# Token stage of a memory-attention gradient: products over two segments at once, with spread weights

## The chip, the cores and the metric

The kernel runs on one core of one Trainium2 chip. The core has five engines that work from queues of their own: TensorE (PE; its weight loads are listed as PEld), VectorE (DVE), ScalarE (ACT), GpSimd (POOL) and SyncE (SP, which here only issues DMAs). The metric is the device time of one execution in microseconds (us), less being better. The kernel before took 5357.48, 5364.2 and 5371.53 us in three runs; the median is 5364.2.

## The reference, cut to what matters

A gated mix of two attentions over 2048 tokens of width 576 is computed, and all its gradients. Attention A has 32 heads of 18 columns with one shared key and value. Attention B works in 64 segments of 32 tokens; each segment sees 8 memory rows ahead of its own tokens, and its output at the memory rows is the memory of the next segment. The change touches B, and in B only the tokens (not the memory rows, which are done in a serial chain elsewhere):

```
for s in range(n_seg):                               # 64 segments of 32 tokens
    xs = x[:, s * seg_len:(s + 1) * seg_len, :]
    h = concatenate([mem, xs], axis=1)               # 8 memory rows + 32 tokens
    q, k, v = einsum('btd,dhe->bhte', h, Wq), ...    # 32 heads of 128
    scores = where(mask, einsum('bhqe,bhke->bhqk', q, k) * scale, -1e9)
    p = softmax(scores)
    o = einsum('bhqe,...', p, v)                     # 'bhqk,bhke->bhqe'
    o = einsum('bhte,hed->btd', o, Wo)
    mem = o[:, :M, :]; outs.append(o[:, M:, :])
...
out = g * a + (1 - g) * b                            # g = sigmoid(x . gate_w)
grads = vjp(grad_out)                                # of x, all weights, mem0, gate_w
```

For the token queries the stage in question computes, head by head, the probabilities P, the output o = P v, and in the gradient dS (the gradient of the scores) and dq = dS k, with the memory rows' share added.

## The kernel before

The program runs in stages that follow each other: preparation; projections of the tokens; the forward chain of memory rows, woven with a pass of attention A; the token stage (`b_bulk`); the backward chain of memory rows, woven with A's second pass; the remaining gradients of B; the weight gradients; the end of A. Only the token stage is touched.

**Its steps.** A step t is four heads of one tile of 128 tokens, that is of four segments; 16 tiles by 8 groups of heads make 128 steps. A step's work is cut into 23 small stages (`st_QT`, `st_S`, `st_R` and so on), which are run as a software pipeline: the list `order` near line 913 holds pairs (n, stage), and turn t of the loop runs each stage in the order of the list for step t - n. There is no scheduler behind it: each engine's queue holds its instructions in exactly the order in which the list calls them. So a stage's place in the list sets its place in each queue that it uses.

**The stages that matter here**, with the engine that does them (the number is that of the list):

- `st_M` (2): DVE clears masked entries of the exponentials x_E.
- `st_QT`, `st_KT` (0), `st_OT` (4), `st_GT` (2), `st_VT` (2): PE transposes four 128x128 blocks of q, k, o, dO, v into a PSUM tile x_tr, of which there are two buffers, used in turn; then DVE (q, k, o) or ACT (dO, v) copies it out as x_qT, x_kT, x_oT, x_dOT, x_vT. PE can begin a transpose once the copy before last has let its buffer go.
- `mem_T`: PE transposes the memory columns of P and dS, DVE copies them out (x_mT).
- `st_B0`, `st_B1` (5): PE multiplies o by the output weights, into x_b.
- `st_R` (2): DVE sums x_E to x_l and inverts to x_r, POOL multiplies x_E by x_r to x_P.
- `st_D` (3): PE forms dO v transposed into x_D; DVE makes x_X (P times it) and its sums x_dl.
- `st_Y` (4): POOL makes x_Y (P times x_dl) and x_dS = x_X - x_Y.
- `st_T` (3) and `st_DT` (5): `transp`, line 741, has DVE transpose the 32x32 blocks of the token part of P and dS to x_PT and x_DT.
- `st_Om`, `st_Qm`: PE multiplies the memory part, one 128x512 product each, into the PSUM tile x_po.
- `st_O` (3) and `st_Q` (5): `attend`, line 764, adds the token part: for each of four heads and each of four segments a product of the segment's 32x32 block by its 32x128 values (v or k), and ACT copies x_po out to x_o or x_dq.

The products of `attend` lie on the diagonal of the PE array: `diag_mm` (line 269) puts segment r in rows and columns 32r to 32r + 32. The blocks of one head stand under each other in x_PT, [128 partitions, 32 columns], so each product takes 32 partitions of it as its weights.

DMAs: SP loads q, k, v, dO every four turns and stores P, dS, o, dq; the stores are collected in a list and issued at the end of the next turn. `self.tmask` (line 173) is a constant of [128, 2, 32] that holds 1 where the segment's number, modulo 2, is the middle index.

Of the kernel before, what the change touches and what calls it, by code (L numbers as in the profile page):

```python
# [10 lines left out]
ALU = mybir.AluOpType  # L11
AX = mybir.AxisListType
BF16 = mybir.dt.bfloat16
# [3 lines left out]
P = 128  # L17
# [29 lines left out]
class Kern:  # L47
# [221 lines left out]
    def diag_mm(self, out, i, lhsT, rhs, start, stop):  # L269
        for r in range(4):  # L270
            b = slice(32 * r, 32 * r + 32)
            self.mm(out[b, i, :], lhsT=lhsT[b], rhs=rhs[b], start=start, stop=stop, tp=(32 * r, 32 * r))

    def m_rows(self, t, c):
        return t[32 * c:32 * c + 8].rearrange("p u e -> p (u e)")
# [388 lines left out]
    def b_bulk(self, wp, vp, kp, sp, psum):  # L664
        nc = self.nc
# [75 lines left out]
        def transp(x, nm):  # L741
            o = sp.tile([P, 4, 32], BF16, name=nm, bufs=2)
            nc.vector.transpose(o[:].rearrange("p i k -> p (i k)"), x.rearrange("p i k -> p (i k)"))
            return o

        def mem_T(t):
            u = [(0, t - 3, "P"), (1, t - 5, "dS")]
# [11 lines left out]
        def attend_m(t, w, m):  # L759
            po = sc["po" + w, t] = psum.tile([P, 4, P], F32, name="x_po", bufs=2)  # L760
            self.mm(po[:].rearrange("p i e -> p (i e)"), lhsT=sc.pop((w + "mT", t)), rhs=m.rearrange("p i e -> p (i e)"),
                    start=True, stop=False)

        def attend(o, t, w, PT, v):
            po = sc.pop(("po" + w, t))
            for i in range(4):
                self.diag_mm(po, i, PT[:, i, :], v[:, i, :], False, True)
            nc.scalar.copy(o, po[:])

        def trans(t, w, nb):  # L770
            tt, g, r, d = view(t)
            pt = psum.tile([P, 4, P], BF16, name="x_tr", bufs=2)
            for i in range(4):
                self.tr(pt[:, i, :], d[w][:, 4 * (g % 4) + i, :], P)
            o = sp.tile([P, 4, P], BF16, name=f"x_{w}T", bufs=nb)
            self.evac(o[:], pt[:], use="s" if w in ("dO", "v") else "v")
            sc[w + "T", t] = o

        st_QT = lambda t: trans(t, "q", 2)
        st_KT = lambda t: trans(t, "k", 2)  # L780
        st_GT = lambda t: trans(t, "dO", 3)
        st_VT = lambda t: trans(t, "v", 3)
# [37 lines left out]
        def st_T(t):  # L820
            sc["PT", t] = transp(view(t)[3]["P"][:, t % 4, 0], "x_PT")

        st_Om = lambda t: attend_m(t, "P", mB["v"][t // 4 % 2][:, t % 4])
        st_Qm = lambda t: attend_m(t, "dS", mB["k"][t // 4 % 2][:, t % 4])

        def st_O(t):
            tt, g, r, d = view(t)
            o = chunk(t, "o", [P, 16, P], 2)
            attend(o[:, r, :], t, "P", sc.pop(("PT", t)), d["v"][:, r, :])
            store(t, self.xtok["o"], o)  # L830
# [11 lines left out]
        def st_B(t, a):  # L842
            tt, g, r, d = view(t)
            oT = sc["oT", t]
            if g == 0 and a == 0:
                pb[tt] = psum.tile([P, 2, 512], F32, name="x_b", bufs=1)
            for i in (2 * a, 2 * a + 1):
                for hf in range(2):
                    self.mm(pb[tt][:, hf, 0:288], lhsT=oT[:, i, :], rhs=self.WoN[:, 4 * g + i, 288 * hf:288 * hf + 288],
                            start=(g == 0 and i == 0), stop=(g == 7 and i == 3))  # L850
            if a == 0:
                return
            sc.pop(("oT", t))
            if g == 7:
                b = sp.tile([P, 2, 288], F32, name="x_bsb", bufs=1)
                nc.scalar.copy(b[:, 0, :], pb[tt][:, 0, 0:288])
                nc.vector.tensor_copy(b[:, 1, :], pb.pop(tt)[:, 1, 0:288])
                due[1].append((self.b_dram[tt * P:(tt + 1) * P, :], b[:].rearrange("p a b -> p (a b)")))

        st_B0 = lambda t: st_B(t, 0)  # L860
        st_B1 = lambda t: st_B(t, 1)
# [22 lines left out]
        def st_DT(t):  # L884
            sc["DT", t] = transp(view(t)[3]["dS"][:, t % 4, 0], "x_DT")

        def st_Q(t):
            tt, g, r, d = view(t)
            dq = chunk(t, "dq", [P, 16, P], 2)
            attend(dq[:, r, :], t, "dS", sc.pop(("DT", t)), d["k"][:, r, :])  # L890
            store(t, self.xtok["dq"], dq)
            if t % 4 == 3:
                C.pop(t // 4)
# [9 lines left out]
        def st_KE(t):  # L903
# [3 lines left out]
            if t % 4 == 3:  # L907
                c2 = t // 4 % 2
                for i in range(4):
                    dst = self.dmx_dram[tt * 32:(tt + 1) * 32].rearrange("m (g i) w e -> i m g (w e)", i=4)  # L910
                    due[1].append((dst[i][:, 4 * c2:4 * c2 + 4, :], dm[32 * i:32 * i + 32].rearrange("p g w e -> p g (w e)")))

        order = [(2, st_M), (0, st_QT), (None, mem_T), (5, st_B0), (0, st_KT), (4, st_Y), (5, st_B1), (4, st_OT),
                 (2, st_R), (2, st_GT), (3, st_T), (5, st_DT), (3, st_Om), (5, st_Qm), (2, st_VT), (1, st_Sm), (3, st_Dm), (1, st_S),
                 (5, st_K), (3, st_D), (5, st_KE), (3, st_O), (5, st_Q)]
        after = {st_O: (("vB", 0), ("v", 0)), st_D: (("mT", 0),), st_KE: (("q", 0), ("dO", 1)), st_Q: (("kB", 0), ("k", 3))}
        later = {}
# [1337 lines left out]
```

## Time and profile before

| what | us |
|---|---|
| median of three runs | 5364.2 |
| the profiled execution, its own time | 5351.38 |
| its span, first to last instruction | 5349.7 |
| PE busy, whole span | 5023.2 (94%) |
| DVE, ACT, POOL busy, whole span | 3619.4, 3323.5, 2421.1 |
| token stage, from its first x_X to its last | 2085.8 to 2663.5 |
| PE, DVE, ACT, POOL busy from 2085 to 2672 | 521.1, 428.7, 366.3, 260.9 |

How to read it: a row of the profile names the source line, the engine, the operation and what it writes and reads (out<-in, buffer numbers left out), its shape, how often, and how long. Where a helper issues the instruction, the line is that of the helper (L82 all matmuls, L87 all transposes of PE, L743 the DVE transposes), so a reader goes by the names of the tiles. An "issue" wait is time in which an engine stands although nothing that the profile shows holds it. Operations of one engine overlap a little at their ends, so what counts on a chain is the time from one start to the next. Some matmul records are missing from the trace (of the products x_po<-x_vmB 35 of 128 are there).

### The profile page before, as it was taken

How to read it: one execution, taken by the hardware profiler on the slowest of the kernel's cores; microseconds unless marked ns; L12 is line 12 of the kernel's file. 1: busy time of each engine (PE TensorE's matmuls, PEld its weight loads, DVE VectorE, ACT ScalarE, POOL GpSimd, SP SyncE). 2: the span in 40 equal slices, each digit the busy share in tenths (PEclk: the TensorE clock that was granted, in tenths of full speed). 3: DMA queues.
4: the chain of work that ended last, by engine and by line, in shares of the span. 5: the costliest groups of instructions: out<-in, count | busy, mean ns of one | idle time of the engine just before them, and what ended most of it. 6: DMA issues, size and time to landing. Idle time of an engine off the chain costs nothing.

```text
span 5349.7 us, 218056 instructions
## 1 busy us (share of the span) xinstructions
PE 5023.2 (94%) x93298; PEld 2941.2 (55%) x93476; DVE 3619.4 (68%) x7146; ACT 3323.5 (62%) x4816; POOL 2421.1 (45%) x4634
## 2 busy tenths in 40 slices
PE   7999999999999998988879999999999999999999
PEld 5434555555555555777735555555554467764444
DVE  5337888888888887777778888888888831111112
ACT  4327888888888886666668888888887732111101
POOL 4004555555555554444436666666654321222223
PEclk9999999999999999999989999999999999999999
DMA  6655655665665445878866889888876679976653
GB/s 217 227 182 131 146 140 143 140 144 144 140 143 131 119 107 181 247 235 241 242 202 170 193 196 199 199 197 200 196 172 140 148 165 224 265 229 210 195 175 114
DMA packets 1115775, 961.45 MB, mean 180 GB/s; under 512 B 690738, under 2 KB 942139, under 8 KB 1105202
## 3 DMA queue, kind: packets, MB, share of 16 engines
q1 hardware_dynamic: 1013730, 702.18, 53.2%
q0 software_dynamic: 100928, 245.16, 15.2%
q8 instruction: 731, 11.98, 1.0%
q14 instruction: 242, 1.98, 0.1%
q10 hardware_dynamic: 144, 0.15, 0.0%
HBM read 521.16 MB, written 357.96 MB: 164 GB/s over the span
## 4 chain that ended last, share of the span: by engine, by line
PE 72%; ACT 9%; issue 9%; POOL 3%; DMA 2%; DVE 1%; SPq 1%; POOLq 0%; ACTq 0%; DVEq 0%
PE w_acc L82 12%; PE r_pj L82 7%; PE b_S L82 6%; PE a_S L82 6%; PE a_acc L82 5%; PE c_pj L82 5%; ACT b_E L1951 5%; PE b_acc L82 5%; PE r_x L82 5%; PE p_pb L82 4%; PE c_x L82 4%; ACT a_E L1778 4%; PE x_tr L87 3%; PE x_b L82 2%; PE x_po L82 2%
## 5 line engine op out<-in xcount | busy, mean ns | idle before, releaser
L1974 DVE TENSOR_TENSOR b_dS<-b_dP,b_E 128x512 bf16<-128x512 f32 x2048 | 1314.3, 683 | 224.7 <-issue 91.1
L1811 DVE TENSOR_TENSOR a_W<-a_dP,a_E 128x512 bf16<-128x512 f32 x2048 | 1313.0, 683 | 206.7 <-issue 76.8
L1951 ACT ACTIVATE b_E<-b_S 128x1024 bf16<-128x1024 f32 x1024 | 1048.8, 1024 | 285.4 <-PE b_dP L82 196.2
L1778 ACT ACTIVATE a_E<-a_S 128x1024 bf16<-128x1024 f32 x1024 | 1049.9, 1025 | 240.0 <-PE a_dP L82 192.7
L82 PEld LDWEIGHTS <-b_QS 32*128 32x128 bf16 (+1 forms) x8192 | 270.3, 92 | 522.8 <-issue 463.5
L82 PE MATMUL r_pj<-WT,r_dT 128*32 128x288 bf16 x12288 | 497.2, 287 | 6.0 <-issue 6.0
L82 PE MATMUL b_S<-b_KV,b_QS 32*128 32x512 bf16 x2048 | 405.1, 383 | 92.7 <-ACT b_E L1951 60.8
L82 PE MATMUL w_acc<-w_d,w_h 128*128 128x512 bf16 (+1 forms) x2352 | 470.9, 379 | 2.5
L82 PE MATMUL a_S<-a_QD,l_KV 32*128 32x512 bf16 x2048 | 399.6, 381 | 42.6 <-ACT a_E L1778 20.5
L82 PE MATMUL b_acc<-b_dS,b_QS 128*32 128x512 bf16 x2048 | 424.4, 393 | 0.2
L82 PE MATMUL a_acc<-a_E,l_VK 128*32 128x256 bf16 x8192 | 412.2, 278 | 5.0
L82 PE MATMUL b_acc<-b_E,b_QS 128*32 128x512 bf16 x2048 | 407.1, 394 | 0.0
L82 PE MATMUL b_dP<-b_KV,b_QS 32*128 32x512 bf16 x2048 | 403.8, 389 | 0.1
L82 PE MATMUL a_dP<-a_QD,l_KV 32*128 32x512 bf16 x2048 | 398.6, 385 | 0.1
L82 PEld LDWEIGHTS <-r_dT 128*32 128x32 bf16 x12288 | 336.4, 97 | 97.6 <-issue 10.6
L82 PEld LDWEIGHTS <-w_h 128*128 128x128 bf16 (+1 forms) x2688 | 230.0, 100 | 258.2 <-issue 6.6
L82 PEld LDWEIGHTS <-l_KV 32*128 32x128 bf16 x4096 | 150.1, 91 | 288.1 <-issue 264.4
L82 PE MATMUL a_acc<-a_W,l_WK 128*32 128x256 bf16 x4096 | 291.3, 273 | 0.4 <-DVE a_W L1811 0.3
L79 ACT CAST w_o<-w_acc 128x512 bf16<-128x512 f32 x54 | 31.6, 586 | 384.2 <-PE w_acc L82 358.7
L77 DVE CAST w_o<-w_acc 128x512 bf16<-128x512 f32 x54 | 37.4, 692 | 335.1 <-PE w_acc L82 307.2
L82 PEld LDWEIGHTS <-l_VK 128*32 128x32 bf16 x8192 | 128.9, 94 | 236.9 <-issue 233.1
L1092 POOL TENSOR_TENSOR r_kb<-r_ks,bmask 128x512 bf16<-128x512 bf16 x176 | 188.7, 1072 | 105.2 <-DMA r_ks<-px_dram 39.8
(482 smaller groups left out, 10609.6 us busy)
## 6 DMA issues: line engine op xcount, KB each, us to landing
b_QS<-qs_dram SPq DMA_DIRECT2D x256, 256.0 KB
dOx_dram<-p_tok SPq DMA_DIRECT2D x16, 1024.0 KB
c_vx<-vx_dram SPq DMA_DIRECT2D x64, 256.0 KB
krow_dram<-c_k POOLq DMA_DIRECT2D x64, 256.0 KB, 3.5
qrow_dram<-c_q POOLq DMA_DIRECT2D x64, 256.0 KB, 4.3
vrow_dram<-c_v POOLq DMA_DIRECT2D x64, 256.0 KB, 6.5
x_q<-qx_dram SPq DMA_DIRECT2D x32, 512.0 KB
x_k<-kx_dram SPq DMA_DIRECT2D x32, 512.0 KB
```

What stands on the lines that cost most here:

```text
L77: nc.vector.tensor_copy(out, in_)
L79: nc.scalar.copy(out, in_)
L82: return self.nc.tensor.matmul(out, lhsT, rhs, start=start, stop=stop, tile_position=tp, skip_group_check=True)
L87: return self.nc.tensor.transpose(out, in_, self.identB[b:b + nrows, b:b + nrows], tile_position=tp)
L1092: nc.gpsimd.tensor_tensor(out=B[:], in0=a[:].unsqueeze(2).to_broadcast([P, 4, 4, SEG]), in1=self.bmask[:, :, 0].unsqueeze(1).unsqueeze(3). ...
L1778: nc.scalar.activation(E_[n][:], S.pop(n)[:], ACT.Exp, scale=SCALEA)
L1811: nc.vector.tensor_tensor(out=W_[n][:, i, :], in0=dP[i][:], in1=E_[n][:, i, :], op=ALU.mult)
L1951: nc.scalar.activation(E_[n][:], S.pop(n)[:], ACT.Exp, scale=SCALEA)
L1974: nc.vector.tensor_tensor(out=D_[n][:, i, :], in0=dP[i][:], in1=E_[n][:, i, :], op=ALU.mult)
```

## The change

Behind each DVE transpose POOL now multiplies the result by the constant mask, with broadcasts: out of [128, 4 heads, 32] it makes [128, 4 heads, 2, 32], in which a segment's block stands in the half that belongs to it and zeros in the other. Two segments under each other are then a 64x64 block-diagonal matrix, and `diag_mm2` multiplies it by the 64x128 values of both in one product: two products for a head instead of four. The result is the same sums with zeros added.

The order of the list changes too: `st_Y`, `st_T` and `st_DT` move up behind `mem_T`, ahead of `st_B0` and `st_KT`. On DVE this puts x_PT and x_DT between x_mT and x_kT, where they were between x_r and x_X. On POOL the order becomes x_Y, x_dS, the two spreads (x_PTB, x_DTB), x_P. The queues of SP and ACT keep their order. The whole program's PE rows go from 186,320 to 182,224, and POOL's from 4547 to 4803.

```diff
+    def diag_mm2(self, out, i, lhsT, rhs, start, stop):
+        for r in range(2):
+            b = slice(64 * r, 64 * r + 64)
+            self.mm(out[b, i, :], lhsT=lhsT[b], rhs=rhs[b], start=start, stop=stop, tp=(64 * r, 64 * r))
...
         def transp(x, nm):
             o = sp.tile([P, 4, 32], BF16, name=nm, bufs=2)
             nc.vector.transpose(o[:].rearrange("p i k -> p (i k)"), x.rearrange("p i k -> p (i k)"))
-            return o
+            B = sp.tile([P, 4, 2, 32], BF16, name=nm + "B", bufs=2)
+            nc.gpsimd.tensor_tensor(out=B[:], in0=o[:].unsqueeze(2).to_broadcast([P, 4, 2, 32]),
+                                    in1=self.tmask[:].unsqueeze(1).to_broadcast([P, 4, 2, 32]), op=ALU.mult)
+            return B[:].rearrange("p i f k -> p i (f k)")
...
             for i in range(4):
-                self.diag_mm(po, i, PT[:, i, :], v[:, i, :], False, True)
+                self.diag_mm2(po, i, PT[:, i, :], v[:, i, :], False, True)
             nc.scalar.copy(o, po[:])
...
-        order = [(2, st_M), (0, st_QT), (None, mem_T), (5, st_B0), (0, st_KT), (4, st_Y), (5, st_B1), (4, st_OT),
-                 (2, st_R), (2, st_GT), (3, st_T), (5, st_DT), (3, st_Om), (5, st_Qm), (2, st_VT), (1, st_Sm), (3, st_Dm), (1, st_S),
+        order = [(2, st_M), (0, st_QT), (None, mem_T), (4, st_Y), (3, st_T), (5, st_DT), (5, st_B0), (0, st_KT), (5, st_B1),
+                 (4, st_OT), (2, st_R), (2, st_GT), (3, st_Om), (5, st_Qm), (2, st_VT), (1, st_Sm), (3, st_Dm), (1, st_S),
                  (5, st_K), (3, st_D), (5, st_KE), (3, st_O), (5, st_Q)]
```

## The prediction

> **What bounds the kernel now.** The page first. Its span is 5349.7 us, and rows 1 and 2 say that PE is busy nearly everywhere. The change touches only the token stage, so the next view is the table by stretches: the stage's 128 steps (16 token tiles by 8 groups of four heads) run from 2085 to 2672 us. The first line below is that stretch, the second a slow piece of it, the third one quiet step.
>
> ```profile
> 2085.00:2672.00 587.00, 521.09 (x14173) 431.85 (x14265) 428.74 (x1414) 366.30 (x780) 260.91 (x404) 0.97 0.81 241
> 2204.00:2209.00 5.00, 4.43 (x45) 3.49 (x45) 1.20 (x4) 1.07 (x2) 0.00 (x0) 0.50 0.58 203
> 2405.24:2409.17 3.93, 3.88 (x123) 3.30 (x119) 3.32 (x11) 2.81 (x7) 1.96 (x4) 1.00 0.91 271
> ```
>
> The columns are PE, PEld, DVE, ACT and POOL busy, the granted clock, the DMA share and GB/s. A quiet step takes 3.93 us and PE is busy for 3.88 of it: PE bounds it, POOL works for half of it. From the first to the last x_X there are 577.6 us for 127 steps, 4.55 each; the median step is 3.98. So about 70 us are lost in some steps. The waits of PE in the stage say where (longest first, us in total, times, longest):
>
> ```profile
> PE x_po L82 <- issue: 17.8, 14, 3.2
> PE x_D L82 <- issue: 16.7, 17, 3.1
> PE x_tr L87 <- issue: 8.4, 5, 2.2
> PE x_tr L87 <- ACT x_dOT L79: 4.5, 15, 0.3
> ```
>
> With the smaller rows, PE stands 52.1 us in waits that no semaphore explains. They come at multiples of 255 rows of PE's program. The page has 186,774 PE and PEld rows and 731 packets on the queue of kind instruction:
>
> ```profile
> q8 instruction: 731, 11.98, 1.0%
> ```
>
> That is one packet for 255.5 rows. In the trace's records of these packets every one of the 34 longer gaps ends 1.3 to 1.5 us after such a packet has landed, on a DMA that is 81% busy. I matched 107 packets with the row at which PE entered the block before: from that entry to the packet's end plus 1.41 us takes 4.5 us in the median, over 5.5 in a quarter of the cases, 8.3 at most. In a quiet step PE uses up a block in 255.5 / 224 rows x 3.93 = 4.48 us, so about half of the blocks come late. A long gap also costs the clock: in the second line above, after 3.17 us of idle, it is 0.50. Seven such stretches, 27.3 us in all, follow gaps of 1.8 us or more; half of that, 13.6 us, is lost.
>
> Last the order of one quiet step, DVE and then PE:
>
> ```profile
> 2405.24 0.42 DVE L871 SCALAR_TENSOR_TENSOR x_X<-x_D,x_P 128x256 f32<-128x256 f32 x1 [0.22 <-PE x_D L82]
> 2405.70 0.42 DVE L874 TENSOR_REDUCE x_dl<-x_X 128x4 f32<-128x256 f32 x1
> 2406.04 0.28 DVE L806 TENSOR_TENSOR x_E<-x_E,maskX 128x128 uint32<-128x128 uint32 x1
> 2406.24 0.42 DVE L77 COPY x_qT<-x_tr 128x512 bf16<-128x512 bf16 x1
> 2406.57 0.28 DVE L757 COPY x_mT<-x_S 128x256 bf16<-128x256 bf16 x1
> 2406.89 0.42 DVE L77 COPY x_kT<-x_tr 128x512 bf16<-128x512 bf16 x1
> 2407.61 0.42 DVE L838 COPY x_oT<-x_tr 128x512 bf16<-128x512 bf16 x1 [0.29 <-PE x_tr L87]
> ...
> 2408.49 0.28 DVE L743 STREAM_TRANSPOSE x_PT<-x_P 128x128 bf16<-128x128 bf16 x1
> 2408.69 0.27 DVE L743 STREAM_TRANSPOSE x_DT<-x_dS 128x128 bf16<-128x128 bf16 x1
> ```
>
> ```profile
> 2405.08 0.40 PE L82 MATMUL x_po<-x_v,x_PT 32*32 32x128 bf16 x16
> 2405.31 0.39 PE L82 MATMUL x_po<-x_k,x_DT 32*32 32x128 bf16 x16
> 2405.64 0.40 PE L87 MATMUL x_tr<-identB,x_q 128*128 128x128 bf16 x4
> ...
> 2407.41 0.39 PE L87 MATMUL x_tr<-identB,x_dO 128*128 128x128 bf16 x4
> ```
>
> The reader is to see three things. From x_X to x_kT DVE works without a gap, 1.65 us from start to start. The transposes of dO write into the x_tr buffer that x_kT reads (two buffers, five users), so PE may start them only after x_kT, which ends at 2407.31; they start at 2407.41, 0.1 us later. And from there to the next x_X (2409.17) PE alone decides: 1.76 us.
>
> **The change part by part.**
>
> *Products (attend).* 32 matmuls and 32 weight loads of a step become 16 and 16; PE's rows a step go from 224 to 192. Today the two groups take 0.23 and 0.32 us start to start. No row shows a 64x64 product. From below: four rounds of 128 columns, as the four transposes of x_tr take 0.22 us: 0.22 + 0.22 = 0.44. From above: the eight do not overlap at all, each 0.055 like one transpose: 0.44 + 0.44, and 0.09 for the change of shape at the end, 0.97. I take 0.5: today's four 32x32 products run side by side in those same rounds. The Trainium skill (TensorEngine Tiling (Array Packing), Key Properties) says that different tiles load and multiply in parallel; no run here shows that for 64x64.
>
> *Transposes moved ahead of x_kT.* x_PT and x_DT go in between x_mT and x_kT. The DVE queue that they pass: x_kT, x_oT, x_l, x_r now stand behind them. In the rows a DVE operation of 0.28 us is followed 0.20 later (x_E to x_qT, x_PT to x_DT). So x_kT starts 0.46 + 0.34 + 0.20 + 0.33 + 3 x 0.20 = 1.93 us after x_X instead of 1.65, ends at 2.35, and PE starts dO 0.05 (the shortest that any step shows) to 0.09 later: 2.40 to 2.44. With 1.76 behind it the loop from x_X to x_X is 4.16 to 4.20 us. That is more than PE's 3.93, so PE now waits before dO, about 0.2 us in each step. Against the median step: 127 x (4.18 - 3.98) = 25 us. It is not paid where PE is late anyway before dO: in the 16 steps that evict x_b (0.67 us of gap each) and for some of the remaining fetch gaps, together about 4 us. **+21 us**; ends +12 (a third is hidden) and +34 (127 x 0.27, against 3.93).
>
> *Spreads on POOL.* Two TENSOR_TENSOR, 128x256 bf16 each, nearest the c_PBm row of the chain stage, 629 ns, and x_P here, 613. POOL's step grows from 1.96 to 3.2 us. In the new order, from x_X: x_dl ends 0.88, x_Y starts 1.03, x_dS 1.72 to 2.45, spreads to 3.15 and 3.85, x_P to 4.55. The P products need the first at 3.94 (4.16 - 0.22), the dS products the second at 4.12, and x_mT's transposes need x_P at about 4.7. All are met, the last by 0.1: I cost them at nothing. The cover is this 0.1 to 0.3 us; a spread of 0.8 instead of 0.63 would make PE wait 0.2 us more a step, 25 us. PE's wait for x_PT changes from DVE to POOL, and behind it in PE's queue stands the whole next step. x_P's writer moves behind the spreads; nobody else waits for it before the next step.
>
> *x_Y moved up.* Its inputs are ready when x_dl ends, and POOL idles ahead of it (134.6 us in the stage), so the place in the list gives nothing. The queues of SP and ACT keep their order; POOL's own 21 DMA issues in the stage (0.5 to 0.8 us each) may stand behind a spread, and nothing in the step waits for them.
>
> *Fewer rows to fetch.* A block now lasts 255.5 / 192 x 4.18 = 5.56 us instead of 4.48. If packets take as long from entry to use as today, what is late is, over the 107 packets, 64.4 us beyond 4.5 and 24.6 beyond 5.55. The gaps seen are 51.9, 0.81 of the first. By the same share, and for 96 blocks, 18 us are left; 192 rows times 4 is 3 blocks, so blocks may last unevenly (4.7, 4.95 and 7.0 us in the worst phase), which leaves 25. I take 22: **-30 us**, ends -20 and -40. Gaps shrink by about 1.1 us each, and of the seven that brought the clock to 0.50 two stay above 1.8: 5 of 7 of 13.6 us, **-8 us** (shrunk for the steps that will not wait on PE), ends -3 and -13.
>
> The Trainium skill (Runtime: NRT & Kernel Launch, Instruction fetch mechanics) says that crossing a 256-instruction block is mostly hidden; by it these two terms are zero and the sum is +21. The trace does not agree: 52.1 us of gaps in this stage alone.
>
> **Sum:** 21 - 30 - 8 = -17 us. The profiled execution itself took 5351.4 us, 1.7 over its span and 12.8 under the median of the runs, 5364.2. I set the sum on the median: **5347 us**.
>
> **Rivals.**
>
> A. *PE does not wait before dO*, since x_kT is not held or the wait falls where PE stands anyway. For it: half of the steps have some gap. Against it: x_kT to dO is 0.09 us in most steps, so there is no room. Then -38, and -2 for shorter products: 5324.
>
> B. *The fetch gaps stay.* What a packet needs could go by the bursts of loads every four steps, and three blocks in four steps could lock onto them; then the same packets are late, however long a block lasts. For it: gaps come in bunches. Against it: every gap follows entry plus packet, and the lateness beyond 5.6 us is small. Then +21 and nothing back: 5385, slower. It decides as soon as less than 21 of the 65 us in gaps and clock come back.
>
> C. *The products run one after the other, or POOL becomes the bound.* Products of 0.97 us make PE's step 3.93 - 0.55 + 0.97 = 4.35, 0.17 over the loop, 22 us, of which longer blocks give back 4: about 5365. With spreads of 0.8 us likewise, 5368. The point: PE over 4.18, that is products over 0.80 us, or spreads over 0.7. A rule bears on the second. The Trainium skill (SBUF — State Buffer, SBUF: two separate sides) says that a POOL operation and a DVE operation with two SBUF inputs block each other. By it a late x_P would hold the mask of x_E, the first step after x_dl, and x_kT with it; no row shows such a hold, since in the times above x_P ends 0.4 us before the mask starts.
>
> **How the numbers follow.** The forecast has 0.55; its own range is -32 to +4 (from -40 - 13 + 21 to -20 - 3 + 27), 5332 to 5368. 0.3%, 16 us, is about what a measurement of this kernel can tell from no change, and -17 lies on that bound: 0.32 of the 0.55 is faster, 0.23 the same. A has 0.10, faster. B has 0.15: 0.12 slower, 0.03 same. C has 0.20: 0.11 slower, 0.09 same (it straddles the bound with the runs' own spread, 5357 to 5372). Together 0.42, 0.35 and 0.23. For 8 in 10 the range must reach A and B: 5326 to 5385.
>
> **What the profile after would show.** Right: the median step at 4.15 to 4.2 us; PE idle before the x_tr transposes of dO with DVE x_kT as releaser, 20 to 25 us in all; issue waits of PE under 30 us; the stage's clock at 0.99; x_PTB and x_DTB near 0.63 us; products at 0.5 us or less. Wrong: issue waits still near 50 (B); PE waiting for POOL (C); median step under 4.1 with no wait for x_kT (A). Anything outside 2085 to 2672 us that moves by over 5 us is outside this account.

## The result and the profile after

The changed kernel takes 5335.86 us in the median of four runs (5332.18 to 5341.36), against 5364.89 for the kernel before in four (5357.48 to 5371.53): a ratio of 0.9949, 95% interval 0.993 to 0.9968. That is 29.0 us less, where 17 less were forecast. Two later comparisons of the same pair (below) gave 17.2 and 22.5 us less; the mean of the three is 23. The profiled execution of the changed kernel took 5334.26 us, its span is 5332.5.

The table by stretches, of the kernel after. The first line is its token stage, the second one quiet step (columns as before: PE, PEld, DVE, ACT, POOL busy, granted clock, DMA share, GB/s).

```profile
2080.00:2636.00 556.00, 524.09 (x12156) 428.17 (x12155) 419.34 (x1415) 361.84 (x773) 409.92 (x647) 1.00 0.85 253
2409.99:2414.12 4.13, 4.09 (x102) 3.38 (x100) 3.22 (x11) 2.82 (x7) 3.14 (x6) 1.00 0.65 205
```

The clock is 1.00 over the whole stage: none of the stretches at 0.50 is left. From the first to the last x_X it takes 551.9 us, 25.7 less than before, although a quiet step takes 4.13 us and not 3.93. POOL's share has grown from 1.96 to 3.14 us a step. The waits of PE from 2085 to 2672 us, the same stretch as before (the stage now ends near 2637, so the rows of the next stage's b_S are left out):

```profile
...
PE x_po L82 <- issue: 6.2, 5, 2.2
PE x_D L82 <- issue: 4.6, 3, 1.6
PE x_tr L87 <- ACT x_dOT L79: 4.5, 15, 0.3
PE x_po L82 <- POOL x_PTB L750: 3.7, 5, 2.5
PE x_b L82 <- issue: 3.0, 3, 1.2
...
PE x_po L82 <- POOL x_DTB L750: 1.1, 5, 0.2
PE x_tr L87 <- DVE x_kT L77: 0.9, 3, 0.3
```

Three things are to be seen. The waits that no semaphore explains, 52.1 us before, are down to some 14. Waits for the new POOL results are small (4.8 us in all, of which 2.5 are one wait in the last steps of the stage). And x_kT, which the prediction named as the releaser of a new wait of 20 to 25 us, is there with 0.9 us only. The packets of instructions have gone down with the rows:

```profile
q8 instruction: 715, 11.71, 1.0%
```

The order of a quiet step, DVE, then PE, then POOL:

```profile
2410.01 0.42 DVE L879 SCALAR_TENSOR_TENSOR x_X<-x_D,x_P 128x256 f32<-128x256 f32 x1 [0.64 <-PE x_D L82]
...
2411.34 0.28 DVE L765 COPY x_mT<-x_S 128x256 bf16<-128x256 bf16 x1
2411.53 0.30 DVE L748 STREAM_TRANSPOSE x_PT<-x_P 128x128 bf16<-128x128 bf16 x1
2411.76 0.27 DVE L748 STREAM_TRANSPOSE x_DT<-x_dS 128x128 bf16<-128x128 bf16 x1
2411.95 0.38 DVE L77 COPY x_kT<-x_tr 128x512 bf16<-128x512 bf16 x1
```

```profile
2409.84 0.41 PE L82 MATMUL x_po<-x_v,x_PTB 64*64 64x128 bf16 x8
2410.09 0.39 PE L82 MATMUL x_po<-x_k,x_DTB 64*64 64x128 bf16 x8
2410.41 0.40 PE L87 MATMUL x_tr<-identB,x_q 128*128 128x128 bf16 x4
...
2411.96 0.39 PE L87 MATMUL x_tr<-identB,x_o 128*128 128x128 bf16 x4
2412.39 0.38 PE L87 MATMUL x_tr<-identB,x_dO 128*128 128x128 bf16 x4
```

```profile
2411.72 0.73 POOL L889 TENSOR_TENSOR x_dS<-x_X,x_Y 128x256 bf16<-128x256 f32 x1
2412.41 0.67 POOL L750 TENSOR_TENSOR x_PTB<-x_PT,tmask 128x256 bf16<-128x256 bf16 x1
2413.03 0.67 POOL L750 TENSOR_TENSOR x_DTB<-x_DT,tmask 128x256 bf16<-128x256 bf16 x1
2413.66 0.61 POOL L825 TENSOR_TENSOR x_P<-x_E,x_r 128x256 bf16<-128x256 bf16 x1
```

x_kT now starts 1.94 us after x_X and ends at 2.32; PE starts dO 0.06 later, 0.43 us after it started o, where these two used to follow each other in 0.22. PE thus stands about 0.2 us in each step. Why the waits of PE do not say so is seen in the weight loads. These are the groups of loads ahead of the dO transposes, from 2085 to 2640 us, of the kernel before:

```profile
L87 PEld LDWEIGHTS <-x_dO 128*128 128x128 bf16 x484 | 33.4, 100 | 2.4 <-issue 2.2
```

and of the kernel after:

```profile
L87 PEld LDWEIGHTS <-x_dO 128*128 128x128 bf16 x503 | 37.9, 96 | 19.8 <-issue 19.2
```

The last columns are the idle time just before and what ended it. In the quiet step above the loads are these:

```profile
2412.13 0.10 PEld L87 LDWEIGHTS <-x_dO 128*128 128x128 bf16 x1
2412.39 0.21 PEld L87 LDWEIGHTS <-x_dO 128*128 128x128 bf16 x3 [0.16 <-issue]
```

One weight load of dO goes ahead, the next ones come only at 2412.39, when x_kT has let the buffer go; so the wait is booked as idle time of the loads, 2.4 us before and 19.8 after, with "issue" as its name.

### The profile page after: what moved, and what is told of

Read it like the earlier page. It is cut to its first block, busy times and chain, and to the rows that moved or that the text cites. A ratio compares the mean times of both kernels' runs of the same rounds, so it can differ in the third digit from the quotient of the medians.

```text
span 5332.5 us, 214646 instructions
## 1 busy us (share of the span) xinstructions
PE 5036.9 (94%) x91428; PEld 2940.1 (55%) x91428; DVE 3610.4 (68%) x7146; ACT 3321.1 (62%) x4816; POOL 2576.9 (48%) x4890
```

## The experiments

The theory behind the forecast: the new order adds a wait of some 0.2 us a step, and 192 rows a step instead of 224 take away more than that, as fewer instruction packets come late. A rival to the second part (B): gaps of PE depend on where the packets fall, not on the number of rows. A rival on the first (C): POOL, or the products themselves, set the step.

For all runs I took the same three numbers from the trace. *Gaps* are the starts of PE groups that follow the one before by over 0.45 us, less the usual 0.2, without the place that recurs at the end of a tile (0.67 us each; 13 of the 15 that the waits show as ACT x_dOT are taken out, 8.8 us in every run). What counts as a group is a matter of choice, so these sums are good to about 1 us. Most gaps have no name in the waits, and such a gap ends 1.2 to 1.7 us after a packet of instructions has landed: in the profile before that holds for all of them, in the first one after for 16 of 21. In e1, e4 and e6 between a quarter and a little over half of the gaps, by time, are not of this kind (below). *Clock loss* is the length of the stretches at 0.50 in the stage, times one half. *Rest* is the span outside the stage, the stage being first to last x_X.

| profiled execution | rows a step | median step | stage | gaps | clock loss | rest |
|---|---|---|---|---|---|---|
| before | 224 | 3.98 | 577.6 | 53.1 | 13.7 | 4772.0 |
| after | 192 | 4.13 | 551.9 | 19.1 | 0.0 | 4780.7 |
| e1_t_after_kt | 192 | 3.95 | 542.9 | 26.7 | 1.7 | 4779.8 |
| e2_one_segment | 224 | 4.17 | 585.2 | 44.3 | 6.8 | 4779.7 |
| e3_order_alone | 224 | 4.20 | 594.1 | 47.4 | 15.4 | 4773.0 |
| e4_third_spread | 192 | 4.15 | 562.3 | 27.2 | 1.7 | 4772.0 |
| e5_changed_again | 192 | 4.13 | 568.1 | 28.5 | 8.5 | 4780.7 |
| e6_after_kt_again | 192 | 3.95 | 530.9 | 16.9 | 1.7 | 4772.2 |
| e7_rows_shifted | 192 | 4.13 | 553.9 | 18.7 | 1.7 | 4772.8 |
| e8_changed_third | 192 | 4.13 | 560.3 | 24.6 | 5.1 | 4765.5 |
| e9_after_kt_third | 192 | 3.95 | 558.1 | 35.9 | 10.2 | 4777.2 |

### The order alone (e3)

The kernel before with nothing but the new list.

```diff
-        order = [(2, st_M), (0, st_QT), (None, mem_T), (5, st_B0), (0, st_KT), (4, st_Y), (5, st_B1), (4, st_OT),
-                 (2, st_R), (2, st_GT), (3, st_T), (5, st_DT), (3, st_Om), ...
+        order = [(2, st_M), (0, st_QT), (None, mem_T), (4, st_Y), (3, st_T), (5, st_DT), (5, st_B0), (0, st_KT), (5, st_B1), (4, st_OT),
+                 (2, st_R), (2, st_GT), (3, st_Om), ...
```

> The kernel before with the new order of the list alone; no spreads, products of one segment on the transposes themselves. My theory: x_kT is 0.25 us later, the median step goes from 3.98 to 4.12-4.18 (18 to 25 us over 127 steps), less about 4 where PE is late anyway; a block lasts 4.70 instead of 4.48 us, which takes 8 to 14 us of the 52 us of gaps and 2 to 5 of the clock's 14. Sum about +5, 5360 to 5380. Rival A, that the order costs nothing: the median step stays at 3.98 and the time at 5365 or below. Rival, that the order is what gained: 5345 or below.

Measured: 5366.0 us (10 runs), ratio 1.0011 (1.0002 to 1.002) to 5361.42 for the kernel before, so 4.6 us more, with an interval of about 1 to 11. In the trace x_kT ends 2.33 us after x_X, dO follows 0.05 later and 1.74 us lead to the next x_X: the same three pieces, to 0.01 us, as in the changed kernel. So the wait comes from the order and needs neither the spreads nor the new products. The gaps stay:

```profile
PE x_po L82 <- issue: 16.6, 15, 2.6
PE x_D L82 <- issue: 13.0, 12, 2.9
PE x_tr L87 <- issue: 5.0, 5, 2.0
PE x_b L82 <- issue: 4.7, 4, 2.7
PE x_S L82 <- issue: 4.5, 5, 1.4
```

The stage of this profiled execution is 16.5 us longer than that of the kernel before; taking out 5.7 us less in gaps and 1.7 more of clock loss, 20.5 are left for the longer steps. Gaps and clock were expected to give back more, 8 to 14 and 2 to 5 us; in this one execution they did not. The medians of the runs show less, 4.6. Part of the difference is that the profiled execution of before (5351.4) lies 12.8 us under its median, and this one (5368.8) 2.8 over its own.

### The spreads and the order, but one segment a product (e2)

The changed kernel, whose products again take one segment each, out of the spread tile: 224 rows a step.

```diff
+    def diag_mmB(self, out, i, lhsT, rhs, start, stop):
+        for r in range(4):
+            b = slice(32 * r, 32 * r + 32)
+            f = slice(32 * (r % 2), 32 * (r % 2) + 32)
+            self.mm(out[b, i, :], lhsT=lhsT[b, f], rhs=rhs[b], start=start, stop=stop, tp=(32 * r, 32 * r))
...
-                self.diag_mm2(po, i, PT[:, i, :], v[:, i, :], False, True)
+                self.diag_mmB(po, i, PT[:, i, :], v[:, i, :], False, True)
```

> The changed kernel in everything (order, spreads on POOL, waits of PE for them), but each product takes one segment again, its 32x32 block cut out of the spread tile: 224 rows of PE a step instead of 192. My theory, that the gain is in the blocks of PE's program: the products take 0.5 to 0.56 us as with two segments, the median step stays at 4.12, a block lasts 4.70 us instead of 5.5, the issue waits of PE go from some 16 us to 33-42 and three to five stretches with the clock at 0.50 come back (4 to 9 us). 5336 + 20 to 32 = 5356 to 5368. Rival, that the gain came from elsewhere (the order, the shorter products themselves, POOL): no more than 5 us of difference, 5336 to 5341.

Measured: 5366.54 us (10 runs), ratio 1.001 (0.9998 to 1.0022), no different from the order alone. Everything of the change is here but the number of products (and with it their shape), and nothing of the gain. The gaps are back at 44.3 us:

```profile
PE x_po L82 <- issue: 13.3, 12, 2.9
PE x_D L82 <- issue: 12.2, 12, 2.3
PE x_tr L87 <- issue: 6.6, 5, 1.6
PE x_b L82 <- issue: 5.4, 3, 2.4
```

The changed kernel stands 17 to 29 us under the kernel before, this one 5 over it: 22 to 34 us for 32 more rows a step (16 matmuls and 16 weight loads), while the three pieces of the loop are the same to 0.01 us, and the two groups of products take 0.23 and 0.32 us, against 0.25 and 0.32 with two segments each, so the shape gains no time. So the gain of the change is its smaller number of instructions.

### A third spread (e4)

The changed kernel with one more POOL operation of the same kind behind the second spread; its result is not used.

```diff
+            if nm == "x_DT":
+                C2 = sp.tile([P, 4, 2, 32], BF16, name=nm + "C", bufs=1)
+                nc.gpsimd.tensor_tensor(out=C2[:], in0=o[:].unsqueeze(2).to_broadcast([P, 4, 2, 32]),
+                                        in1=self.tmask[:].unsqueeze(1).to_broadcast([P, 4, 2, 32]), op=ALU.mult)
```

> The changed kernel with a third POOL operation of the spreads' kind a step, behind them and ahead of x_P; its result is used by nobody. My theory, that POOL has cover: POOL's step goes from 3.2 to 3.9 us, x_P ends 4.9 us after x_X, PE stands 0.2 to 0.3 us before the transposes of P but gets it back before dO, where it would wait for x_kT; median step 4.12 to 4.2, 5336 to 5348. Rival, that POOL is the bound already: every step longer by one such operation, 0.63 us, 127 times: 5415. In between, with the mask of x_E held behind x_P: 0.2 to 0.4 us a step, 5360 to 5385.

Measured: 5347.81 us (10 runs), ratio 0.9977 (0.9964 to 0.999): about 10 us more than the changed kernel (6 to 15 by its ratios of 0.9949 to 0.9965, which come from other comparisons), at the upper edge of what was expected. POOL is now busy for 487 of the stage's 564 us, and a wait of PE for x_P appears:

```profile
PE x_po L82 <- issue: 8.3, 9, 1.8
PE x_tr L87 <- ACT x_dOT L79: 4.5, 15, 0.3
PE x_S L87 <- POOL x_P L829: 4.3, 8, 0.8
```

With 0.62 us more on POOL the median step is 4.15 instead of 4.13, and PE waits for x_P in 8 places. With the waits for the spreads (3.8 and 1.1 us) and for the third one (0.5) PE stands 9.7 us for POOL, against 5.1 in the changed kernel. So the cover of the two spreads in the changed kernel is not 0.1 to 0.3 us but about 0.5: from x_P's end (4.26 us after x_X) to the transpose of x_P (0.62 after the next x_X, or 4.74) there are 0.48. What goes beyond it hardly shows in a quiet step: the transposes of x_P start 0.75 us after x_X instead of 0.63, and from o to dO there are 0.30 instead of 0.43, so PE gets the 0.13 back out of the wait for x_kT.

### The transposes behind x_kT (e1, e6, e9)

The changed kernel, with `st_T` and `st_DT` put behind `st_KT`: the wait of each step should go and the rest stay.

```diff
-        order = [(2, st_M), (0, st_QT), (None, mem_T), (4, st_Y), (3, st_T), (5, st_DT), (5, st_B0), (0, st_KT), (5, st_B1),
+        order = [(2, st_M), (0, st_QT), (None, mem_T), (4, st_Y), (5, st_B0), (0, st_KT), (3, st_T), (5, st_DT), (5, st_B1),
```

> The changed kernel, with the two DVE transposes (and so the spreads) called behind st_KT instead of ahead of it. My theory, that the step is set by the loop x_X to x_kT to the transposes of dO to x_X: x_kT ends 2.08 us after x_X again instead of 2.33, PE waits for it no more, and the median step falls from 4.12 to 3.93-3.98 us, 18 to 24 us over 127 steps. Blocks of PE's program then last 5.25 us instead of 5.5, so 2 to 8 us more of gaps. Sum 10 to 20 us less than the changed kernel: 5316 to 5326. Rival, that POOL's longer step sets the pace and x_kT only follows: the median step stays at 4.12 and the time at 5336.

Measured: 5333.65 us (5 runs), ratio 0.9952 (0.9938 to 0.9965). The step did what was expected, the time less: it missed the range by 8 us. Its gaps are of another kind, too. In 12 turns ACT waits for the store of an earlier x_o to land, which sets the buffer free, and PE, which transposes x_o, waits for ACT; the first profile of the changed kernel has neither row:

```profile
ACT x_o L776 <- DMA ox_dram<-x_o: 19.4, 12, 4.0
...
PE x_tr L87 <- ACT x_o L776: 9.8, 9, 2.2
```

The second and third comparison put it beside the changed kernel on one chip each:

> The changed kernel once more, on one chip beside the next two, to compare them with each other: 5330 to 5342, fetch gaps near 16 us, median step 4.12.

> The kernel with the transposes behind x_kT once more beside the changed one. My theory: the token stage, from its first to its last x_X, is 5 to 12 us shorter than in the changed kernel (it was 542.9 against 551.9), and the time follows: 5322 to 5335, below the changed kernel on the same chip. Rival: what the step saves comes back in later blocks and in the loads, and the two are equal within 3 us.

Measured: the changed kernel 5334.29 us (12 runs; ratio 0.9965, 0.9952 to 0.9979), with the transposes behind x_kT 5330.35 (7 runs; 0.9961, 0.9948 to 0.9974). The profiled execution of the changed kernel has gaps of 28.5 us (issue waits of some 24), where 16 were expected. Its stage is 37 us longer than the other's, where 5 to 12 were expected.

> The changed kernel a third time, beside the next on one chip: 5325 to 5342; its token stage, first to last x_X, between 550 and 570 us.

> The kernel with the transposes behind x_kT a third time. The profiled stages so far are 542.9 and 530.9 us against 551.9, 568.1 and 553.9 of the changed kernel, 20 us less in the mean, and the medians only 2 to 4 us less. My theory: the stage is again 10 to 30 us shorter and the median 5 to 15 us lower than that of the changed kernel on this chip. Rival: the medians are within 4 us, and what the stage gains in the profiled executions is not seen in the others.

Measured: the changed kernel 5339.29 us (11 runs; 0.9955, 0.9939 to 0.997), the other 5328.39 (6 runs; 0.9936, 0.9915 to 0.9958). The median is lower by 10.9 us, as forecast; the stage of the profiled execution is only 2.2 us shorter (558.1 against 560.3), where 10 to 30 were forecast. (Of the three stages that the expectation gives for the changed kernel, 553.9 is that of the kernel with the rows shifted, below.)

The step, DVE and then the weight loads of dO (from 2085 to 2640 us), in e6:

```profile
2409.63 0.42 DVE L879 SCALAR_TENSOR_TENSOR x_X<-x_D,x_P 128x256 f32<-128x256 f32 x1 [0.81 <-PE x_D L82]
...
2410.96 0.28 DVE L765 COPY x_mT<-x_S 128x256 bf16<-128x256 bf16 x1
2411.28 0.42 DVE L77 COPY x_kT<-x_tr 128x512 bf16<-128x512 bf16 x1
2411.62 0.30 DVE L748 STREAM_TRANSPOSE x_PT<-x_P 128x128 bf16<-128x128 bf16 x1
2411.84 0.27 DVE L748 STREAM_TRANSPOSE x_DT<-x_dS 128x128 bf16<-128x128 bf16 x1
```

```profile
L87 PEld LDWEIGHTS <-x_dO 128*128 128x128 bf16 x504 | 33.7, 98 | 0.2 <-issue 0.2
```

The next x_X is at 2413.56, 3.93 us on. The idle time before the loads of dO is 0.2 us, after 19.8 in the changed kernel: it was x_kT that held them, and DVE's order that held x_kT. This settles the cause of the longer step.

The time is settled less well. The two comparisons on one chip differ by 3.9 and 10.9 us in the medians, 8.1 and 10.0 in the means of all runs, with standard errors of 4.9 and 4.6; weighted, 9 us, 95% interval about 3 to 16. 127 steps times 0.18 would be 23. Over three profiled executions each the stage is 16 us shorter (544.0 against 560.1). So some 40 to 70 in a hundred of a wait on PE's path became time. One reason the traces show: part of what the step saves comes back as waits for the stores of x_o, 9.8 us of PE in e1; in e6 ACT waits for them 3 times, 5.3 us, and in e9 not at all. Another is near at hand and was not shown: where PE stands anyway in a gap, the wait had cost nothing. That a shorter step uses up a block of instructions sooner (255.5 rows in 5.26 us, not 5.50) does not show: its three profiled executions have gaps of 26.7, 16.9 and 35.9 us, those of the changed kernel 19.1, 28.5 and 24.6, 2 us more in the mean and more scatter than that; and the gaps that follow a packet of instructions are 11.6, 9.0 and 33.1 us of the first and 16.7, 26.1 and 21.5 of the second. Of the versions measured this is the one to keep; that it is faster than the kernel before is shown three times, that it is faster than the changed kernel only in these two comparisons taken together. A third buffer of x_tr, which would take the wait away at its root, was not tried.

### The rows shifted (e7)

If gaps depended on where blocks of instructions begin in the step (rival B: three blocks in four steps), they would change when all rows of the stage are moved against the blocks. Ahead of the loop PE makes 32 transposes of a constant, 64 rows, whose results are not used.

```diff
+        for _ in range(8):
+            ps = psum.tile([P, 4, P], BF16, name="x_tr", bufs=2)
+            for i in range(4):
+                self.tr(ps[:, i, :], self.identB[:], P)
         for t in range(NG + 6):
```

> The changed kernel with 32 transposes of the identity (64 rows of PE, 2 us, result unused) once ahead of the token stage, so that every block of PE's program begins 64 rows, a third of a step, elsewhere. My theory, that a late block is a matter of how long a block lasts: gaps between 10 and 28 us instead of 16, the time between 5330 and 5350. Rival, that three blocks in four steps happen to miss the bursts of loads in the changed kernel and would meet them in another phase: gaps of 40 us or more and 5360 or more.

Measured: 5329.67 us (4 runs), ratio 0.9962 (0.9948 to 0.9976), gaps of 18.7 us against 19.1, 28.5 and 24.6 in the three profiled executions of the changed kernel. The time lies 0.3 us below the expected range, the gaps inside it. A move by 64 rows, a quarter of a block, does not bring the gaps back; the changed kernel did not just fall into a lucky place.

Where the gaps fall is another matter, and there B's idea has something in it. Counted from the first x_X, the three profiled executions of the changed kernel all have gaps in steps 38, 42, 46, 62, 74, 93 and 117, mostly a multiple of four apart, and SP issues its loads every four turns; in e9 20.2 of the 33.1 us that follow packets lie in one step of every four. With the rows shifted the places are others (37, 41, 49, 57, 61 and so on), the sum is as before. So the four-turn rhythm seems to choose the block that is late (the loads were not moved, so this is not shown), and how long a block lasts to decide what it costs.

## Why the prediction was right

Its sign and its path held, and so did each of its three terms in the mean of the profiled executions; the sum came out 6 us short of the mean of the three comparisons and 12 short of the first. By the traces the terms are +19 for the step, -24 for the gaps and -8 for the clock (below), -13 together, where the medians show -17 to -29; the last point says where the rest may lie.

- **The longer step, +21.** Forecast: x_kT ends at 2.35, dO starts 0.05 to 0.09 later, 4.16 to 4.20 a step. Measured: 2.33, 0.05, then 1.74 where 1.76 was taken; 4.12 to 4.13. The median step grows from 3.98 to 4.13, 127 x 0.15 = 19 us. The x_kT term was shown twice, by the order alone (it appears) and by the transposes behind x_kT (it goes). What failed is the sign to look for: the profile does not name DVE's x_kT as releaser, 0.9 us instead of 20 to 25; the time stands as idle time of the weight loads under "issue", 19.8 us.
- **Fewer rows, -30.** Measured 53.1 - 19.1 = 34 us in the first pair. With 192 rows the eight profiled executions have gaps of 16.9 to 35.9 us, 24.7 in the mean; with 224 rows the three have 44.3 to 53.1, 48.3. The estimate of 22 left was close to that mean. The runs e2 (rows back, gain gone) and e7 (rows moved, gain stays) rule out B as it was forecast, that the same packets stay late and nothing comes back. The Trainium skill (Runtime: NRT & Kernel Launch, Instruction fetch mechanics) has the crossing of blocks mostly hidden; in this stage it is not, and 32 rows less a step are worth 22 to 34 us.
- **The clock, -8.** 13.7 us of loss before, 0.0 in the first profiled execution after, 0 to 10.2 in all with 192 rows, 3.8 in the mean, against 12.0 in the three with 224. So 8 fits the means; in the first pair the term was short by 6, which lies within the scatter of 0 to 10.2. The reading that a gap of 1.8 us brings the clock down is too simple: in the changed kernel's first profile PE stands 2.2 us until 2406.18, and no stretch at 0.50 follows.
- **The products, 0.5 us.** Start to start the two groups take 0.25 and 0.32, or 0.57, where sixteen 32x32 products took 0.23 and 0.32. The value was low by 0.07; it cost nothing, since PE waits for x_kT later in the step. Eight products of 0.055 each one after the other would be 0.44 a group: at 0.25 the two on the diagonal run side by side, if one takes as long as a transpose with the same 128 columns. The Trainium skill (TensorEngine Tiling (Array Packing), Key Properties) says the same, that different tiles load and multiply in parallel.
- **The spreads, at nothing.** 0.67 us each, not 0.63, but one starts 0.62 after the other, since the ends overlap. The cover was given as 0.1 to 0.3 us and is 0.48. Rival C put the point where POOL decides at 0.7 us a spread; the third spread shows that for the quiet step it lies near 0.93 for each of the two (0.62 us more for both together moved the median step by 0.02), though the whole took some 10 us more by then.
- **The hold of DVE by POOL, and POOL's DMA issues.** In a quiet step the mask of x_E starts 0.80 us after x_X, when x_P has ended, so these steps can't show the hold that rival C speaks of. Four steps of the changed kernel show it. There two DMA issues of POOL (1.04 to 1.07 us together) stand ahead of x_Y, the POOL chain is late, and x_P and the mask start together; first DVE, then POOL:

```profile
2136.17 0.42 DVE L882 TENSOR_REDUCE x_dl<-x_X 128x4 f32<-128x256 f32 x1
2136.50 0.72 DVE L814 TENSOR_TENSOR x_E<-x_E,maskX 128x128 uint32<-128x128 uint32 x1
```

```profile
2136.45 0.62 POOL L825 TENSOR_TENSOR x_P<-x_E,x_r 128x256 bf16<-128x256 bf16 x1
```

The mask takes 0.71 to 0.75 us in these four instead of 0.28, and ends some 0.15 us after x_P. It does so, or is held for a part, in every profile with the spreads and in neither of the two without. With the third spread x_P ends 0.77 us after the next x_X, just ahead of the mask, so only six masks of that run are long (0.41 to 0.78). DVE's x_dl (0.42 us), which reads one tile, and x_X (0.42), of whose two one lies in PSUM, keep their time beside POOL's operations. The prediction had no row for the hold and took the DMA issues to cost nothing, since nothing in the step waits for them. In each of the four steps PE waits 0.3 us for x_PTB and 0.2 for x_DTB: 2 us in all, so the term stays near nothing.

- **Rival A** is out too: the wait is there in all five kernels that have the new order.
- **The base.** The terms came from one execution of 5351.4 us and were set on the median 5364.2. In the first pair the stage gave back 25.7 us and the rest of the span took 8.7 (4780.7 against 4772.0), which leaves 17, the difference of the spans (5349.7 and 5332.5); the medians differ by 29.0. Whether the 12.8 us that the profiled execution was faster than its median would have stood in the same gaps was not measured; if so, the row term is larger for the median than for that execution, and the missing 6 to 12 us may lie there.

## What to carry to other kernels

Where PE's program is long and has gaps that no semaphore explains, count its rows per us: fewer instructions can be worth more than shorter ones, even if each step gets longer, and the packets on the queue of kind instruction show it. Before an operation is moved up in an engine's queue, follow what it passes to the buffer it lets go (here x_kT to x_tr to dO), and test the two halves of such a change apart: here the order cost and the row count paid. Look for a small wait in the starts of the groups and in the idle time of the weight loads, as a wait of 0.2 us a step may not be named. And look at the longest, not only the median, of an operation that begins beside one of POOL: the hold of the mask is in 4 of 128 steps.

## What the runs showed of the hardware that was not expected

- DVE's mask of x_E, with both inputs in SBUF, takes 0.71 to 0.75 us instead of 0.28 where it begins beside POOL's x_P, and ends some 0.15 us after it.
- A wait of PE of 0.2 us for a buffer is not listed under its releaser but as "issue" of the weight loads (19.2 us in 127 steps).
- Two 64x64 products on the diagonal take as long as four of 32x32: 0.25 and 0.32 us for eight matmuls of 128 columns, 0.23 and 0.32 for sixteen.
- The part of the program that the change does not touch takes 4765.5 to 4780.7 us. The part ahead of the stage moves little (2082.8 to 2087.5), the part behind it from 2681.2 to 2697.8, in no relation to the kernel (the changed one has both the least and the most). Clock loss there goes from 41.4 to 55.5 us, 41.4 in the shortest and 51.8 in the longest, but does not order the runs between. The spread of 15 us is as large as half the effect measured here, so a change of one stage is better read from that stage than from one span.
